# A decode step on one core: 256 rows of w4 as eight four-row loads ahead of w3

## The chip, the cores and the metric

One core of a Trainium2 chip runs the whole program. The metric is the device time of one execution in microseconds; the median of three runs of the kernel before is 193.53 us (193.38 to 193.78).

## The reference

A pre-norm block for one new token of eight sequences: attention over the last 2048 cached positions, and an MLP. Only these lines matter (`_B_ref` with S = 1 makes the shifted branch `hs` zero, so w1 and w2 are not read):

```python
# attention: q from x (8x512) by wq (512x4096); 32 heads, 8 kv heads, W = 2048 of 8192 positions
scores = einsum("bhqd,bhkd->bhqk", q, k) * Dh ** -0.5
o = einsum("bhqk,bhkd->bhqd", softmax(scores), v).reshape(B, Sq, Hq * Dh) @ wo
# MLP: w3 is 512x1792, w4 is 1792x512
h2 = gelu(layernorm(x1) @ w3) @ w4        # x1 = x + 0
# whole
h = x + attention(layernorm(x)); out = h + B_ref(layernorm(h))
```

All tensors are bf16. The key and value caches that are read make 67 MB of the 79 MB.

## The kernel before

Every engine has its own list of operations (`PE`, `AC`, `DV`, `PO`, `SP`), written out by hand in the order in which they are recorded; an operation waits on the counts of others or on a load's semaphore. All large loads go out on SyncE's queue in one order: wq, then 32 loads of keys and values of 2 MB (128 rows of 16 KB), four loads of wo of 1 MB, two of w3 (`sem_w3`), four of w4 (`sem_w4`), all through the helper at L199. Keys and values go through a ring of eight slots in SBUF (`ring`); a load into a slot waits until TensorE has taken what was there. w3 and w4 go into two slots of that ring.

Per slot of keys TensorE transposes (L325), ScalarE and VectorE evict (L334, L336), and TensorE makes the scores (L345). The softmax of one sequence is spread over following steps; GpSimd expands the probabilities (L384). The values are multiplied at L445, and after the last sequence at L454.

The tail is written in this order. `reorder` (L534 to L540) places the attention's output for the product with wo. `pe_wo` (L548) makes that product in four parts, one for each load of wo. Between them `stream(n)` (L596) has TensorE run n products that nobody reads, 512 columns wide. Sums for the layer norm follow (L685 to L700), then `uT`, the input of the MLP, whose tile GpSimd clears at L684. The product with w3 (L710) is made in two halves, one for each load of w3, over 14 chunks of 128 features; the results lie in two PSUM tiles, 8 chunks 64 columns wide and 6 chunks 32 wide. VectorE scales them (`g_x`, L738), ScalarE applies the GELU (`gT`, L741). TensorE adds the residual into the output's PSUM tile (`pe_fin`, L747), then the product with w4 (L755): two products for a chunk, side by side in two column groups of TensorE. Eviction (L775, L776) and the store (L779) end the program.

w4 is loaded in groups of 8, 3, 2 and 1 rows per partition, so that a group of r rows serves r chunks:

```python
w4_chunks += [slice(f0 + i, f0 + 128 * r, r) for i in range(r)]
dma(SP, w4_sb[:, lo:lo + r, :].rearrange("p r n -> p (r n)"),
    B_w4[f0:f0 + 128 * r, :].rearrange("(p r) n -> p (r n)", r=r), sem, w_free[1] if lo == 0 else None)
```

x_sb, the eight rows of the input, is loaded on ScalarE's queue by itself, the output is stored on SyncE's.

Of the kernel before, what the change touches and what calls it, by code (L numbers as in the profile page):

```python
# [11 lines left out]
B = 8  # L12
D = 512
# [9 lines left out]
FC = F // 128  # L23
KC = D // 128
EPS = 1e-5

NS = 8
NKT = 3
# [39 lines left out]
def bass_sequential_preLN__sliding_block_cached__mixer_s_mlp__decode_kernel(  # L68
# [23 lines left out]
    with es:  # L92
        sb = lambda shape, dtype, name: es.enter_context(nc.sbuf_tensor(name, shape, dtype))
        ps_t = lambda shape, dtype, name: es.enter_context(nc.psum_tensor(name, shape, dtype))
        S = lambda name: es.enter_context(nc.semaphore(name))
# [4 lines left out]
        ident_b = sb([128, 128], dt.bfloat16, "ident_b")  # L100
# [16 lines left out]
        QH, RW = H // 8, 8  # L117
# [12 lines left out]
        P4_sb = sb([128, 512, 4], dt.bfloat16, "P4_sb")  # L130
# [17 lines left out]
        half = sb([128, 2], dt.float32, "half")  # L148
# [38 lines left out]
        O_ps, O2_ps = (ps_t([128, 512], dt.float32, n) for n in ("O_ps", "O2_ps"))  # L187
# [3 lines left out]
        sem_wo = [S(f"sem_wo{i}") for i in range(NWO)]  # L191
        sem_x, sem_wq, sem_out = (S(n) for n in ("sem_x", "sem_wq", "sem_out"))
        sem_w3 = [S(f"sem_w3{i}") for i in range(2)]
        sem_w4 = [S(f"sem_w4{i}") for i in range(4)]
# [64 lines left out]
        e = PE.op(pe_xT, e_xln, e_idb)  # L259
# [22 lines left out]
        e = PE.op(pe_qT, *e_qr)  # L282
# [18 lines left out]
        place = {l: n for n, l in enumerate(quads)}  # L301
        taken = {}
# [123 lines left out]
        e_acc, e_oT = {}, {}  # L426
# [75 lines left out]
        v3 = lambda t: t.rearrange("p (n b) -> p n b", b=B)  # L502
        vr = lambda t: t.rearrange("p (n b) -> p b n", b=B)

        def bc(t):
            a = t[:, :]
            return bass.AP(tensor=a.tensor, offset=a.offset, ap=[a.ap[0], [0, KC], [1, B]])
# [82 lines left out]
            if p >= 7 + LQK + 7 and (p - 7 - LQK - 7) % 8 == 0:  # L590
                softmax_5((p - 7 - LQK - 7) // 8)

        def stream(n):
            def f(e):
                for _ in range(n):
                    ins = e.matmul(O2_ps[:, :], ident_b[:, :], kT_sb[:, (NG - 1) % NKT, 0:512], start=True, stop=True)  # L596
                return ins
            if n:
                PE.op(f, e_acc[NV - 4])
# [37 lines left out]
        pick_rest(14, 1)  # L637
        finish(13)
        pick_rest(14, 2, 3)
        stream(4)  # L640
        pv(60)
        finish(14)
        pv(61, 62, 63)

        e_oR = reorder()
        stream(3)
        for n in range(NWO):
            pe_wo(n, e_oR, e_oz)
            stream((0, 4, 4, 1)[n])


        dma(SP, wq_v, A_wq.rearrange("(p k) n -> p k n", k=KC), sem_wq)
        for l in loads:
            what, b, j = l
            if what == "wo":
                n, qh = b, QH // NWO
# [4 lines left out]
            n = place[l]  # L661
# [4 lines left out]


        w_free = [taken[quads[n - NS]] for n in (len(quads), len(quads) + 1)]
        for a, sem in enumerate(sem_w3):
            dma(SP, w3_sb[:, 2 * a:2 * (a + 1), :].rearrange("p r f -> p (r f)"),  # L670
                B_w3[256 * a:256 * (a + 1), :].rearrange("(p r) f -> p (r f)", r=2), sem, w_free[0])

        FH = 8
        w4_chunks, w4_ends, f0 = [], [], 0
        for r, sem in zip((8, 3, 2, 1), sem_w4):
            lo = len(w4_chunks)
            w4_chunks += [slice(f0 + i, f0 + 128 * r, r) for i in range(r)]
            dma(SP, w4_sb[:, lo:lo + r, :].rearrange("p r n -> p (r n)"),
                B_w4[f0:f0 + 128 * r, :].rearrange("(p r) n -> p (r n)", r=r), sem, w_free[1] if lo == 0 else None)
            w4_ends.append(lo + r)  # L680
            f0 += 128 * r
        assert len(w4_chunks) == FC

        e_uz = PO.op(lambda e: e.memset(uT, 0.0), e_PT[LAST, 3])  # L684
        e_d = DV.op(lambda e: e.tensor_tensor(v3(hd[:, :]), hT, v3(xc[:, :]), ALU.add), e_wo[-1], e_xc[0])  # L685
# [6 lines left out]
        e_u = DV.op(lambda e: e.scalar_tensor_tensor(uT[:, :, 0:B], bc(msum), -1.0 / D, v3(hd[:, :]),  # L692
                                                     ALU.mult, ALU.add), e_ms, e_uz)
# [9 lines left out]
        y_ps, NY = [kbank[0], kbank[2]], (64, 32)  # L703

        def pe_w3(half, lo, hi, *waits):
            def f(e):
                for fc in range(lo, hi):
                    n, f = divmod(fc, FH)
                    for kc in (2 * half, 2 * half + 1):
                        ins = e.matmul(y_ps[n][:, f * NY[n]:(f + 1) * NY[n]], w3_sb[:, kc, w4_chunks[fc]],  # L710
                                       uT[:, kc, 0:NY[n]], start=(kc == 0 and f == 0), stop=(kc == KC - 1),
                                       skip_group_check=True)
                return ins
            return PE.op(f, *waits)
        pe_w3(0, 0, FC, e_u, (sem_w3[0], 16), e_scale[LAST, 1], e_acc[NV - 2])
        stream(1)
        e_y = [pe_w3(1, 0, FH, (sem_w3[1], 16)), pe_w3(1, FH, FC)]

        e = AC.op(lambda e: e.activation(s2[:, :], vsum[:, :], ACT.Sqrt, bias=eps2[:, :], scale=(1.0 + EPS) / D), e_vs)  # L719
        e1 = AC.op(lambda e: e.activation(s1[:, :], vsum[:, :], ACT.Sqrt, bias=eps1[:, :], scale=1.0 / D))  # L720
# [14 lines left out]
        for n in range(2):  # L735
            fn = (FH, FC - FH)[n]
            cs = slice(n * FH * B, (n * FH + fn) * B)
            e = DV.op(lambda e, n=n, cs=cs, fn=fn: e.tensor_tensor(v3(g_x[:, cs]),   # L738
                y_ps[n][:, 0:fn * NY[n]].rearrange("p (f w) -> p f w", w=NY[n])[:, :, 0:B], bcf(r2, fn),
                                                                   ALU.mult), e_y[n], e_r2)  # L740
            e_gT.append(AC.op(lambda e, cs=cs: e.activation(gT[:, cs], g_x[:, cs], ACT.Gelu_apprx_tanh), e))  # L741
        z_ps = S_ps[1]

        def rows(e, w, rhs, start=False, stop=False):
# [6 lines left out]
        def pe_w4(lo, hi, *waits):  # L751
            def f(e):
                for fc in range(lo, hi):
                    for a in range(2):
                        ins = e.matmul(z_ps[64 * a:64 * a + B, 0:256], gT[:, fc * B:(fc + 1) * B],  # L755
                                       w4_sb[:, fc, 256 * a:256 * (a + 1)].rearrange("p (j r) -> p r j", r=2),
                                       start=False, stop=(fc == FC - 1), tile_position=(0, 64 * a), skip_group_check=True)
                return ins
            return PE.op(f, *waits)

# [4 lines left out]
            return ins  # L765

        PE.op(pe_fin, e_fin, e_exp[LAST], e_scale[LAST, 1])
        stream(2)
        for n, hi in enumerate(w4_ends):
            e_z = pe_w4(w4_ends[n - 1] if n else 0, hi, (sem_w4[n], 16), e_gT[0 if hi <= FH else 1])  # L770
        e_out = []
        for a in range(2):
            src = z_ps[64 * a:64 * a + B, 0:256].rearrange("p (r j) -> p r j", r=2)
            dst = out_sb[:, 256 * a:256 * (a + 1)].rearrange("p (j r) -> p r j", r=2)
# [38 lines left out]
```

## Time and profile before

| | |
|---|---|
| median of 3 runs | 193.53 us (193.38 to 193.78) |
| the profiled execution | 193.76 us, its span 192.3 us |
| TensorE busy, products / weight loads | 159.8 us (2108) / 101.8 us (2108) |
| VectorE, ScalarE, GpSimd busy | 103.8, 84.4, 35.8 us |
| HBM read | 79.18 MB, 412 GB/s over the span |
| granted TensorE clock | 1.0 throughout |

The span is the profiled part of the execution; the rest of its time lies around it. Times in the profile's rows are microseconds from the span's start. A row of instructions gives the line of the kernel, the engine, the operation, output and inputs, and in brackets the idle time ahead of it with what ended it.

### The profile page before, as it was taken

What the parts mean: (1) busy time and instruction counts of PE and PEld (TensorE: products, weight loads), DVE (VectorE), ACT (ScalarE), POOL (GpSimd) and SP (SyncE); (2) the same over time, 40 slices, a digit from 0 to 9 for tenths busy, and PEclk for the clock granted to TensorE, in tenths of its full rate; (3) what the DMA queues carried; (4) which work ended last, traced back from release to release, by engine and by line L of the source; (5) the groups of instructions that cost most, each with busy time, mean ns of one, the idle gap of its engine ahead of it and who ended that gap; (6) DMA issues with size and microseconds to landing.
All of it is one profiled execution on the core that took longest, in us unless ns stands there. A gap on an engine that the chain in (4) does not pass through costs nothing.

```text
span 192.3 us, 4741 instructions
## 1 busy us (share of the span) xinstructions
PE 159.8 (83%) x2108; PEld 101.8 (53%) x2108; DVE 103.8 (54%) x256; ACT 84.4 (44%) x102; POOL 35.8 (19%) x44
## 2 busy tenths in 40 slices
PE   0028999789998989998999797979998998898795
PEld 0015767567665555655656464646565653366472
DVE  7702656367457654665475546554765456552050
ACT  5002776946744544454444532454445423530040
POOL 8000000350520080008000800052004402400000
PEclk9999999999999999999999999999999999999999
DMA  6999999999999999999999999999999999999992
GB/s 220 436 423 436 433 416 433 426 428 423 436 429 433 429 433 423 426 429 431 433 423 433 429 433 429 429 433 426 424 426 429 429 433 433 423 416 430 418 381 77
DMA packets 6244, 79.47 MB, mean 413 GB/s; under 512 B 705, under 2 KB 849, under 8 KB 1361
## 3 DMA queue, kind: packets, MB, share of 16 engines
q1 hardware_dynamic: 6208, 79.18, 97.0%
q8 instruction: 16, 0.26, 0.5%
q10 hardware_dynamic: 16, 0.01, 0.0%
q14 instruction: 4, 0.02, 0.0%
HBM read 79.18 MB, written 0.01 MB: 412 GB/s over the span
## 4 chain that ended last, share of the span: by engine, by line
DMA 78%; PE 16%; DVE 2%; SPq 2%; issue 1%; ACT 0%
DMA ring<-in_A_k_cache_dram 63%; DMA ring<-in_B_w_dram 16%; PE kT_ps L325 8%; PE O_ps L445 3%; PE S_ps L345 3%; SPq L199 2%; DVE kT_sb L336 1%; PE sm L394 1%; PE sm L496 1%; DVE pT_sb L407 1%; PE S_ps L755 0%; DVE mcol L356 0%; ACT P_sb L775 0%; PE sm L360 0%; PE sm L370 0%
## 5 line engine op out<-in xcount | busy, mean ns | idle before, releaser
L334 ACT ACTIVATE kT_sb<-kT_ps 128x1024 bf16<-128x1024 bf16 x64 | 65.2, 1023 | 65.4 <-PE kT_ps L325 65.4
L325 PE MATMUL kT_ps<-ident_p,ring 128*128 128x128 bf16 x1024 | 68.3, 220 | 9.0 <-DMA ring<-in_A_k_cache_dram 7.6
L336 DVE COPY kT_sb<-kT_ps 128x1024 bf16<-128x1024 bf16 x64 | 44.3, 692 | 48.9 <-PE kT_ps L325 48.9
L325 PEld LDWEIGHTS kT_ps<-ident_p,ring 128*128 128x128 bf16 x1024 | 57.7, 98 | 22.5 <-DMA ring<-in_A_k_cache_dram 10.5
L384 POOL TENSOR_TENSOR P_sb<-P_sb,mask_b 128x512 bf16<-128x512 bf16 x30 | 31.2, 1070 | 129.2 <-ACT P_sb L374 120.1
L445 PE MATMUL O_ps<-ring,pT_sb 128*64 128x512 bf16 x208 | 31.6, 390 | 0.0
L345 PE MATMUL S_ps<-kT_sb,qwin 128*32 128x512 bf16 x256 | 26.0, 390 | 0.0
L345 PEld LDWEIGHTS S_ps<-kT_sb,qwin 128*32 128x32 bf16 x256 | 6.8, 93 | 16.3 <-issue 14.4
L394 PE MATMUL sm<-ident_s,P_sb 128*128 128x128 bf16 x120 | 11.6, 219 | 2.0 <-DVE pT_sb L407 0.7
L407 DVE COPY pT_sb<-sm 128x512 bf16<-128x512 bf16 x28 | 11.6, 415 | 1.1 <-PE sm L394 1.1
L445 PEld LDWEIGHTS O_ps<-ring,pT_sb 128*64 128x64 bf16 x208 | 7.7, 108 | 6.1 <-issue 1.6
L394 PEld LDWEIGHTS sm<-ident_s,P_sb 128*128 128x128 bf16 x120 | 7.7, 97 | 4.5 <-issue 3.6
L480 DVE SCALAR_TENSOR_TENSOR acc<-O_ps,own_f,acc 128x128 f32<-128x128 f32 x24 | 8.4, 350 | 0.8
L268 PE MATMUL S_ps<-wbig,xlnT 128*32 128x512 bf16 x32 | 3.4, 596 | 5.3 <-DMA wbig<-in_A_wq_dram 5.3
L374 ACT ACTIVATE P_sb<-S_ps,negcol 128x512 bf16<-128x512 f32 x8 | 5.5, 687 | 3.0 <-DVE negcol L373 3.0
L254 PE MATMUL sm<-ident_b,xln_b 8*128 8x8 bf16 x4 | 0.3, 174 | 7.6 <-DVE xln_b L223 7.6
L496 PEld LDWEIGHTS sm<-sum_f,acc 128*128 128x128 f32 x20 | 3.0, 188 | 6.3 <-DVE pT_sb L407 3.3
L356 DVE TENSOR_REDUCE mcol<-S_ps 128x1 f32<-128x512 f32 x8 | 5.5, 689 | 1.5 <-PE S_ps L345 1.5
L480 DVE SCALAR_TENSOR_TENSOR iota_f<-O_ps,own_f,iota_f 128x128 f32<-128x128 f32 x15 | 5.2, 348 | 1.5 <-ACT iota_f L483 1.2
L596 PE MATMUL O_ps<-kT_sb,ident_b 128*128 128x512 bf16 x21 | 5.8, 379 | 0.0
L435 DVE TENSOR_TENSOR oT_all<-sm,rL 128x16 bf16<-128x16 f32 x15 | 3.4, 229 | 4.4 <-PE sm L496 4.3
L719 ACT ACTIVATE s<-vsum,eps 128x8 f32<-128x8 f32 x1 | 0.3, 301 | 11.8 <-DVE vsum L699 11.8
(123 smaller groups left out, 109.8 us busy)
## 6 DMA issues: line engine op xcount, KB each, us to landing
ring<-in_A_k_cache_dram SPq DMA_DIRECT2D x16, 2048.0 KB, 30.7
ring<-in_A_v_cache_dram SPq DMA_DIRECT2D x16, 2048.0 KB, 26.8
wbig<-in_A_wq_dram SPq DMA_DIRECT2D x1, 4096.0 KB, 12.3
wbig<-in_A_wo_dram SPq DMA_DIRECT2D x4, 1024.0 KB, 29.9
ring<-in_B_w_dram SPq DMA_DIRECT2D x2, 896.0 KB, 34.9
ring<-in_B_w_dram SPq DMA_DIRECT2D x1, 1024.0 KB, 32.1
ring<-in_B_w_dram SPq DMA_DIRECT2D x1, 384.0 KB, 30.3
ring<-in_B_w_dram SPq DMA_DIRECT2D x1, 256.0 KB, 30.5
```

The costliest lines, as they stand in the source:

```text
L325: ins = e.matmul(kT_ps[m % 3][:, c * 128:(c + 1) * 128], ring[:, s, n * DH:(n + 1) * DH], ident_p[:, :], is_transpose=True)
L334: e_lo[i] = AC.op(lambda e: e.activation(kT_sb[:, i % NKT, 0:1024], kT_ps[2 * i % 3][:, :], ACT.Copy), e_Tlo[i], e_QK.get(i - NKT))
L336: e_hi[i] = DV.op(lambda e: e.tensor_copy(kT_sb[:, i % NKT, 1024:2048], kT_ps[(2 * i + 1) % 3][:, :]), e_Thi[i], e_QK.get(i - NKT))
L345: ins = e.matmul(S_ps[b % 2][32 * h:32 * (h + 1), :], qwin[:, b, 4 * j + h, w0:w0 + 32], kT_sb[:, i % NKT, :].rearrange("p (c h k) -> p h ...
L356: e_max[b] = DV.op(lambda e: e.tensor_reduce(mcol[:, :], S_ps[b % 2][:, :], AX.X, ALU.max), e_QK[8 * b + 7], e_mT.get(b - 1))
L374: e_exp[b] = AC.op(lambda e: e.activation(P_sb[:, :], S_ps[j][:, :], ACT.Exp, bias=negcol[:, j:j + 1], scale=1.0, accum_out=lcol[:, j:j + 1]),
L384: e_sp[b, r] = eng.op(lambda e, r=r, pb=pb, mb=mb: e.tensor_tensor(P4_sb[:, 128 * r:128 * (r + 1), :], pb, mb, ALU.mult), e_exp[b], e_PT.g ...
L394: ins = e.matmul(buf[:, x * 128:(x + 1) * 128], P4_sb[:, 32 * c:32 * (c + 1), :].rearrange("p k h -> p (k h)"), ident_s[:, :], is_transpos ...
L407: e_pT[b, r] = DV.op(lambda e: e.tensor_copy(dst, pT_ps[:, :]), e_PT[b, r], free)
L445: ins = e.matmul(bank(w)[64 * t:64 * (t + 1), :], pT_sb[:, b % NB3, c, 64 * j:64 * (j + 1)], ring[:, s, :].rearrange("p (a c d) -> p c a d ...
L480: e_part[w] = eng.op(lambda e: e.scalar_tensor_tensor(dst, src, own, dst, ALU.mult, ALU.add), e_part[w], e_PV[4 * w + 3])
L596: ins = e.matmul(O2_ps[:, :], ident_b[:, :], kT_sb[:, (NG - 1) % NKT, 0:512], start=True, stop=True)
```

## The change

A free ring slot (that of the last load of keys) takes 256 of w4's 1792 rows, the first ones, laid out over 64 partitions with eight rows each. GpSimd first clears that area and makes a small selection matrix `near` from the identity. Eight loads of four partitions (8 KB each) then fill the rows, on SyncE's queue between wo and w3: load n writes partitions p, p+4, p+8, p+12 with p = 32(n // 4) + n mod 4. 32 of the 64 partitions are filled so; the others stay zero. The remaining 1536 rows of w4 come in groups of 5, 4, 2 and 1 rows per partition.

The product with w3 now has three PSUM parts: the two chunks for the first 256 features, the five of w4's first group, the other seven. Of the first part, g is put into the layout of the new rows by 16 small products (`pe_near`) and a copy (`gn`), and the product with these rows is eight pairs of TensorE products, placed behind those of w4's first group. The filler products become 128 columns wide, in other numbers; the one between the halves of w3 goes from one to three of 512, and the two ahead of w4 go.

```diff
-        def stream(n):
+        def stream(n, w=512):
...
-        stream(4)
+        stream(12, 128)
         pv(60)
...
         e_oR = reorder()
-        stream(3)
+        stream(12, 128)
         for n in range(NWO):
             pe_wo(n, e_oR, e_oz)
-            stream((0, 4, 4, 1)[n])
+            stream((0, 14, 16, 4)[n], 128)
...
+        side = ring[:, place["k", LAST, 1] % NS, :]
+        near_sb = side[0:64, 0:RW * D].rearrange("p (r n) -> p r n", r=RW)
+        near = side[:, RW * D:RW * (D + 32)].rearrange("p (r n) -> p r n", r=RW)
+        e_nz = PO.op(lambda e: e.memset(near_sb, 0.0), taken["k", LAST, 1])
+        e = PO.op(lambda e: e.memset(near, 0.0))
+        e_near = PO.op(lambda e: e.tensor_copy(near[:, :, 0:16], ident_b[:, :].rearrange("p (n r) -> p r n", r=RW)), e)
+        for n in range(RW):
+            p, f = 32 * (n // 4) + n % 4, 128 * (n // 4) + RW * (n % 4)
+            dst = near_sb[p:p + 13:4].rearrange("p r n -> p (r n)")
+            a = B_w4[f:f + RW, :]
+            dma(SP, dst, bass.AP(tensor=a.tensor, offset=a.offset, ap=[[4 * RW * D, 4], [1, RW * D]]), sem_near, e_nz)
         for a, sem in enumerate(sem_w3):
             dma(SP, w3_sb[:, 2 * a:2 * (a + 1), :].rearrange("p r f -> p (r f)"),
...
-        for r, sem in zip((8, 3, 2, 1), sem_w4):
+        for r, sem in zip((5, 4, 2, 1), sem_w4):
...
+        w3_parts = ((0, NN, 64), (NN, w4_ends[0], 64), (w4_ends[0], FC, 32))
...
-        pe_w3(0, 0, FC, e_u, (sem_w3[0], 16), e_scale[LAST, 1], e_acc[NV - 2])
-        stream(1)
-        e_y = [pe_w3(1, 0, FH, (sem_w3[1], 16)), pe_w3(1, FH, FC)]
+        for n in range(3):
+            pe_w3(0, n, e_u, (sem_w3[0], 16), e_scale[LAST, 1], e_acc[NV - 2])
+        stream(3)
+        e_y = [pe_w3(1, n, (sem_w3[1], 16)) for n in range(3)]
...
+        gn_ps = kbank[1][0:64, 0:RW * B]
+        gn = P4_sb[0:64, 64:80, :].rearrange("p k h -> p (k h)")
+
+        def pe_near(e):
+            for r in range(RW):
+                for t in range(NN):
+                    ins = e.matmul(gn_ps[32 * t:32 * (t + 1), r * B:(r + 1) * B], near[:, r, :], gT[:, t * B:(t + 1) * B],
+                                   start=True, stop=True, tile_position=(0, 32 * t), skip_group_check=True)
+            return ins
...
         PE.op(pe_fin, e_fin, e_exp[LAST], e_scale[LAST, 1])
-        stream(2)
+        e = PE.op(pe_near, e_gT[0], e_near)
+        e_gn = DV.op(lambda e: e.tensor_copy(gn, gn_ps), e, e_PT[LAST, 3])
         for n, hi in enumerate(w4_ends):
-            e_z = pe_w4(w4_ends[n - 1] if n else 0, hi, (sem_w4[n], 16), e_gT[0 if hi <= FH else 1])
+            e_z = pe_w4(gT, w4_sb, w4_ends[n - 1] if n else NN, hi, (sem_w4[n], 16), e_gT[1 if n == 0 else 2])
+            if n == 0:
+                pe_w4(gn, near_sb, 0, RW, e_gn, (sem_near, 16 * RW))
```

More of the change, by code (lines that the diff above doesn't have):

```diff
@@ L193, in bass_sequential_preLN__sliding_block_cached__mixer_s_mlp__decode_kernel @@
         sem_w3 = [S(f"sem_w3{i}") for i in range(2)]
+        sem_near = S("sem_near")
         sem_w4 = [S(f"sem_w4{i}") for i in range(4)]
@@ L591, in bass_sequential_preLN__sliding_block_cached__mixer_s_mlp__decode_kernel @@
                 softmax_5((p - 7 - LQK - 7) // 8)
-        def stream(n):
+        def stream(n, w=512):
             def f(e):
                 for _ in range(n):
-                    ins = e.matmul(O2_ps[:, :], ident_b[:, :], kT_sb[:, (NG - 1) % NKT, 0:512], start=True, stop=True)
+                    ins = e.matmul(O2_ps[:, 0:w], ident_b[:, :], kT_sb[:, (NG - 1) % NKT, 0:w], start=True, stop=True)
                 return ins
@@ L671, in bass_sequential_preLN__sliding_block_cached__mixer_s_mlp__decode_kernel @@
                 B_w3[256 * a:256 * (a + 1), :].rearrange("(p r) f -> p (r f)", r=2), sem, w_free[0])
-        FH = 8
-        w4_chunks, w4_ends, f0 = [], [], 0
-        for r, sem in zip((8, 3, 2, 1), sem_w4):
+        NN = 2
+        w4_chunks, w4_ends, f0 = [slice(128 * i, 128 * (i + 1)) for i in range(NN)], [], 128 * NN
+        for r, sem in zip((5, 4, 2, 1), sem_w4):
             lo = len(w4_chunks)
@@ L678, in bass_sequential_preLN__sliding_block_cached__mixer_s_mlp__decode_kernel @@
             dma(SP, w4_sb[:, lo:lo + r, :].rearrange("p r n -> p (r n)"),
-                B_w4[f0:f0 + 128 * r, :].rearrange("(p r) n -> p (r n)", r=r), sem, w_free[1] if lo == 0 else None)
+                B_w4[f0:f0 + 128 * r, :].rearrange("(p r) n -> p (r n)", r=r), sem, w_free[1] if lo == NN else None)
             w4_ends.append(lo + r)
@@ L701, in bass_sequential_preLN__sliding_block_cached__mixer_s_mlp__decode_kernel, with pe_w3 @@
                                                       ALU.mult, ALU.add))
-        y_ps, NY = [kbank[0], kbank[2]], (64, 32)
-        def pe_w3(half, lo, hi, *waits):
+        y_ps = [sm[:, 128:128 + 64 * NN], kbank[0], kbank[2]]
+        def pe_w3(half, n, *waits):
+            lo, hi, w = w3_parts[n]
             def f(e):
                 for fc in range(lo, hi):
-                    n, f = divmod(fc, FH)
                     for kc in (2 * half, 2 * half + 1):
-                        ins = e.matmul(y_ps[n][:, f * NY[n]:(f + 1) * NY[n]], w3_sb[:, kc, w4_chunks[fc]],
-                                       uT[:, kc, 0:NY[n]], start=(kc == 0 and f == 0), stop=(kc == KC - 1),
+                        ins = e.matmul(y_ps[n][:, (fc - lo) * w:(fc - lo + 1) * w], w3_sb[:, kc, w4_chunks[fc]],
+                                       uT[:, kc, 0:w], start=(kc == 0 and fc == lo), stop=(kc == KC - 1),
                                        skip_group_check=True)
@@ L734, in bass_sequential_preLN__sliding_block_cached__mixer_s_mlp__decode_kernel @@
         e_gT = []
[L735 to L739, printed above, removed]
+        for n, (lo, hi, w) in enumerate(w3_parts):
+            cs = slice(lo * B, hi * B)
+            e = DV.op(lambda e, n=n, cs=cs, fn=hi - lo, w=w: e.tensor_tensor(v3(g_x[:, cs]),
+                y_ps[n][:, 0:fn * w].rearrange("p (f w) -> p f w", w=w)[:, :, 0:B], bcf(r2, fn),
                                                                    ALU.mult), e_y[n], e_r2)
             e_gT.append(AC.op(lambda e, cs=cs: e.activation(gT[:, cs], g_x[:, cs], ACT.Gelu_apprx_tanh), e))
+        gn_ps = kbank[1][0:64, 0:RW * B]
[6 more added lines that the diff above has]
+            return ins
         z_ps = S_ps[1]
@@ L749, in rows, with pe_w4 @@
             return ins
-        def pe_w4(lo, hi, *waits):
+        def pe_w4(g, w, lo, hi, *waits):
             def f(e):
@@ L754, in f @@
                     for a in range(2):
-                        ins = e.matmul(z_ps[64 * a:64 * a + B, 0:256], gT[:, fc * B:(fc + 1) * B],
-                                       w4_sb[:, fc, 256 * a:256 * (a + 1)].rearrange("p (j r) -> p r j", r=2),
-                                       start=False, stop=(fc == FC - 1), tile_position=(0, 64 * a), skip_group_check=True)
+                        ins = e.matmul(z_ps[64 * a:64 * a + B, 0:256], g[:, fc * B:(fc + 1) * B],
+                                       w[:, fc, 256 * a:256 * (a + 1)].rearrange("p (j r) -> p r j", r=2),
+                                       start=False, stop=(w is w4_sb and fc == FC - 1), tile_position=(0, 64 * a), skip_group_check=True)
                 return ins
```

## The prediction

> **What bounds the kernel now.** First the page: its transfers by slice and the chain that ended last.
>
> ```profile
> span 192.3 us, 4741 instructions
> DMA  6999999999999999999999999999999999999992
> GB/s 220 436 423 436 433 416 433 426 428 423 436 429 433 429 433 423 426 429 431 433 423 433 429 433 429 429 433 426 424 426 429 429 433 433 423 416 430 418 381 77
> DMA 78%; PE 16%; DVE 2%; SPq 2%; issue 1%; ACT 0%
> ```
>
> The kernel is a stream of 79 MB at about 430 GB/s, and the chain is 78% transfers. A change pays only if the last bytes land earlier and TensorE is then ready for them. The last two slices, 381 and 77 GB/s, are not full. The table of busy time by windows shows why (last columns: granted clock, DMA share of 16 engines, GB/s):
>
> ```profile
> 186.00:186.50 0.50, 0.50 (x12) 0.50 (x11) 0.00 (x0) 0.00 (x0) 0.00 (x0) 1.00 1.02 404
> 186.50:187.00 0.50, 0.50 (x18) 0.47 (x18) 0.23 (x1) 0.00 (x0) 0.00 (x0) 1.00 0.60 242
> 187.00:188.00 1.00, 0.90 (x13) 0.29 (x14) 0.21 (x1) 0.50 (x2) 0.00 (x0) 1.00 0.59 227
> 188.00:189.00 1.00, 1.00 (x16) 0.61 (x16) 0.00 (x0) 0.00 (x0) 0.00 (x0) 1.00 0.50 185
> 189.00:189.50 0.50, 0.36 (x8) 0.18 (x6) 0.00 (x0) 0.00 (x0) 0.00 (x0) 1.00 0.40 143
> ```
>
> From 186.5 us half of the DMA engines have nothing left, while the other half work on until about 190. Every load gives each engine the same bytes, so something else holds that half back. The table of queues names it:
>
> ```profile
> q1 hardware_dynamic: 6208, 79.18, 97.0%
> q8 instruction: 16, 0.26, 0.5%
> q10 hardware_dynamic: 16, 0.01, 0.0%
> q14 instruction: 4, 0.02, 0.0%
> ```
>
> q8 has 16 packets of 16 KB of instructions. The trace's single packets show that one takes 0.88 to 0.97 us of its engine and slows the packet behind it. On one engine a packet begins some 4 ns before the last one ends, so I could follow each engine: the fetches go round eight engines, two each, and make those some 2.9 us late; a ninth, with two 8 KB packets of q14, is about 1.7 us late; seven are free or nearly. The sixteen landings of the last load, w4's last 128 KB, agree: seven at 186.7 to 187.5 us, one at 188.36, eight at 189.6 to 190.12.
>
> The TensorE timeline (weight loads: start, length) shows what the late eight hold up:
>
> ```profile
> 185.57 1.35 PEld L710 LDWEIGHTS kT_ps<-P_sb,ring 128*128 128x128 bf16 x28 [0.66 <-DMA ring<-in_B_w_dram]
> 187.99 0.77 PEld L755 LDWEIGHTS S_ps<-ring,gT 128*8 128x8 bf16 x16 [0.59 <-DMA ring<-in_B_w_dram]
> 189.20 0.21 PEld L755 LDWEIGHTS S_ps<-ring,gT 128*8 128x8 bf16 x6 [0.44 <-DMA ring<-in_B_w_dram]
> 189.82 0.09 PEld L755 LDWEIGHTS S_ps<-ring,gT 128*8 128x8 bf16 x4 [0.41 <-DMA ring<-in_B_w_dram]
> 190.13 0.09 PEld L755 LDWEIGHTS S_ps<-ring,gT 128*8 128x8 bf16 x2 [0.22 <-DMA ring<-in_B_w_dram]
> ```
>
> Each group of w4 products waits for its load; the last pair starts at 190.13, 0.01 us after the last landing. All behind it (eviction, store) is unchanged.
>
> **The change: where the bytes go.** x_sb is a load of eight rows; its queue q10 has 16 packets: eight of data, eight that count the semaphore. So a load of eight rows uses eight engines, and one of four rows should use four. Then the eight new loads put 64 KB on each of four engines: 8 packets of 8 KB at 0.305 us (0.309 each, 4 ns of overlap) and 8 semaphore packets at 5 ns, 2.48 us. The other loads of w4 shrink from 14 to 12 KB per partition, 8 partitions an engine: 16 KB less on every engine, 0.61 us by the spacing of 16 KB packets (0.611 less 0.004). So twelve engines end 0.61 us earlier, the four 2.48 - 0.61 = 1.87 us later. If the four are free ones, they end at 187.46 + 1.87 = 189.33 at most, the late ones at 190.12 - 0.61 = 189.51, which is the new last landing.
>
> [...]
>
> **Issue.** The new loads wait on POOL: its last product of L384 ends at 165.3, then a memset of 64x4096 (3.29 us for 128x3840 at L213, so 3.5), end 168.8. uT's memset, queued behind it and two short ones, moves from 167.4 to about 169.5; it is needed at 183.3. On SP the w3 and w4 issues queue behind the wait: eight at 0.48 us (spacing of the wo issues) to 172.7, the six others to about 176, if the queue takes them (it held one back 11 us before, with ten loads outstanding). The free engines finish wo at 178.0. Cost nothing; cover 2 us for the last issue, 9 us for the first; without it each us late is a us lost.
>
> **TensorE.** On late engines w3's second half still lands at 185.56, the new loads not being theirs. stream(3) before it takes 3 x 0.213 = 0.64 from 184.84, so 185.48: hidden, by 0.08. The other fillers become 128 wide: 12 to 16 at 0.05 to 0.06 us against 3 or 4 at 0.213, no longer than before and each in front of a load it waits for anyway; nothing. Then, by starts in the rows of before: y, 14 products of 64 columns at 0.060 and 14 of 32 at 0.0255, to 186.80 (186.87 before); pe_fin's eight to 187.1. The 16 products that place g aren't in the trace: lower bound L534 (same 32-column weights, 0.35 us for 32, so 0.18 for 16), upper bound 0.96 (0.060 each, as y's). I take 0.2, L534 having the same form. Their copy starts 0.26 later (as L738 behind y) and takes 0.21 and 0.05 to be seen: 187.8. Meanwhile five pairs of w4's first group (landed at 187.98 before, with 24 KB or 0.9 us more per engine, so 187.1 now), at 0.113 a pair (spacing at L755): 187.3 to 187.9. Then 8 + 4 + 2 + 1 = 15 pairs, the new eight included; the last starts 14 x 0.113 = 1.58 later, at 189.5. That is level with the landing at 189.51, and all the removed waits of L755 are filled. At the upper bound it is 190.2 and nothing is gained; with 0.1 to 0.2 us of unseen semaphore time, 189.7.
>
> **Sum.** The last pair moves from 190.13 to 189.53 (transfers) or 189.7 (TensorE): 0.43 to 0.60 us, I take 0.5. The profiled execution took 193.76 us (span 192.3 and 1.4 around it), 0.23 over the median of 193.53; on it 193.26, on the median 193.0.
>
> **Rivals.**
> *One of the four carries fetches (slower).* Of the eight engines that took x_sb's rows, my tracking gives five free or nearly, one with q14's two packets, two with q8's two. Which four a four-row load takes, the trace doesn't say. For: by blind choice it would be likely. Against: the two with q8 come next to each other in the round of eight and may as well be at the far end of the order. It decides as soon as one of the four is late by over 0.2 us. With a q8 engine w3's second half lands at 185.56 + 2.48 = 188.04; the whole TensorE tail moves by as much, last pair 192.05: +1.9, 195.4 us. With the q14 engine it lands at 183.98 (its landing before) + 2.48 = 186.46, 0.9 later; last pair 190.4 to 190.6: 193.9.
> *The tail stays where it is.* TensorE has 70 products more (42 fillers, 16 to place g, 12 for the new rows), each with a weight load: 4216 + 140 = 4356 instructions. The 16 fetches came about every 256, so a 17th falls due at 4352, in the last products. Lag from that count to the packet was 2.7 us in the last two, which puts it past the end; where it comes sooner it holds a late engine by up to 1 us. With that, or placing g nearer its upper bound, 0 to 0.35 us is left: 193.2 to 193.5.
> [...]
> *Small loads cost one by one (slower).* If each new load paid a round trip (the store's 0.9 us from issue to landing), eight would take 7.2 us on the four engines: 186.7 + 7.2 - 0.61 = 193.3 for their end, +3.2, 196.7. Against: the semaphore packets of queued loads take 9 ns, and the next data follows with no gap.
> [...]
> *The loads spread over all sixteen.* Then no engine gains, w3 lands 0.6 later, TensorE's last pair is at 190.1 to 190.3: 193.6. x_sb's packets speak against it.
>
> **How the numbers follow.** Forecast 0.52; q8 engine 0.14; q14 engine 0.11; tail 0.15; cost one by one 0.03; spread 0.05. The forecast's own range is 192.9 to 193.15. 192.8 (lowest run 193.38 less 0.6) to 194.2 takes in all but the q8 engine and the cost one by one. About 0.2%, 0.39 us, is what a measurement of this kernel can tell from no change: faster by more 0.52 (the forecast), within 0.20 (tail, spread), slower 0.28.
>
> **What would show it.** Right: the share of DMA engines stays at about 1.0 to past 188.5 and drops steeply; w3's second half is taken up at 185.6 and no w4 group waits long; the last pair starts near 189.5. Wrong: L710's second half starting at 186.5 or 188 (a loaded engine was late already), a DMA share of a quarter or less trailing past 190, a 17th q8 packet before 189.5, or the copy of g starting after 188.2. Gaps between packets before 186 us would mean that the issues came too late.

## The result and the profile after: slower by about a microsecond

The changed kernel takes 194.59 us (median of 6 runs, 194.30 to 195.12) against 193.59 for the kernel before in the same runs (6, 193.38 to 193.78). The ratio is 1.0057 [1.0039, 1.0075]: slower, where 193.0 was forecast, and above the range given. The profiled execution took 194.56 us. Two kernels further down (e13, e14) had executions 3 to 4 us longer at a lower granted clock, and their ratios leave these out.

The page of the changed kernel, its transfers by slice, its chain and its queues:

```profile
span 192.9 us, 4897 instructions
DMA  6999999999999999999999999999999999999981
GB/s 219 435 431 435 428 425 431 425 426 428 428 431 428 431 428 428 435 418 430 431 428 428 428 431 435 425 435 426 425 421 435 435 428 431 425 415 426 423 362 48
q1 hardware_dynamic: 6272, 79.18, 96.7%
q8 instruction: 17, 0.28, 0.5%
q14 instruction: 3, 0.02, 0.0%
DMA 44%; PE 40%; DVE 5%; POOL 4%; ACT 3%; SPq 3%; issue 1%
```

The last two slices have become emptier (362 and 48 GB/s, from 381 and 77): the end did not fill up. The chain now goes 40% through TensorE, but it is one path among several of nearly equal length, and most of the difference lies far ahead of the change. Queue q8 has its 17th packet; by the single packets it begins at 188.90 us.

The table of busy time by windows (last columns: granted clock, DMA share, GB/s):

```profile
186.00:186.50 0.50, 0.49 (x3) 0.00 (x0) 0.00 (x0) 0.00 (x0) 0.00 (x0) 1.00 0.77 315
187.00:187.50 0.50, 0.50 (x20) 0.50 (x17) 0.17 (x1) 0.16 (x1) 0.00 (x0) 1.00 0.75 309
188.50:189.00 0.50, 0.50 (x10) 0.23 (x6) 0.16 (x1) 0.00 (x0) 0.00 (x0) 1.00 0.50 170
189.00:189.50 0.50, 0.50 (x12) 0.38 (x12) 0.00 (x0) 0.00 (x0) 0.00 (x0) 1.00 0.06 25
190.00:190.50 0.50, 0.50 (x12) 0.39 (x12) 0.00 (x0) 0.00 (x0) 0.00 (x0) 1.00 0.03 10
```

This has two signatures at once. From 186 to 188 us the share is 0.73 to 0.78, about twelve engines, where before it was 0.60 from 186.5 on, nine or ten: four engines got new rows, but only about three of them had been idle. And a share of 0.06 is one engine of sixteen, and it goes on alone from 189 to past 190. The sixteen landings of w4's last load show the same: four at 186.2 to 186.5 us, eleven at 188.48 to 189.40, one at 190.58. Before there were seven early ones, a single one at about 188.3 and eight late ones. Less the 0.61 us by which w4's loads shrank, the single one would stand at 187.7; none does. So three of the four loaded engines were early ones, and the fourth is the one that stood alone.

The timeline of the changed kernel (a row of products, then weight loads: start, length) shows what that one engine held up on its way:

```profile
184.75 0.28 PE L724 MATMUL sm<-P_sb,ring 128*128 128x64 bf16 x4 [1.11 <-DMA ring<-in_B_w_dram]
186.80 0.17 PEld L724 LDWEIGHTS sm<-P_sb,ring 128*128 128x128 bf16 x4 [0.81 <-DMA ring<-in_B_w_dram]
188.35 0.43 PEld L778 LDWEIGHTS S_ps<-ring,gT 128*8 128x8 bf16 x10
189.01 0.77 PEld L778 LDWEIGHTS S_ps<-ring,P_sb 64*8 64x8 bf16 x16 [0.23 <-issue]
190.01 0.69 PEld L778 LDWEIGHTS S_ps<-ring,gT 128*8 128x8 bf16 x14 [0.23 <-issue]
```

L724 is the product with w3 (L710 before). Its second half is taken up at 186.80 us, 1.23 later than before, and waits for a transfer: fifteen of its sixteen landings are there by 185.54 and the last at 186.76. Its first half, too, waits until 184.75, for a last landing at 184.61. w4's first group starts at 188.35, its last landing being at 188.30. From there TensorE has no wait left. The last seven pairs start at 190.01, so the last of them, six spacings of 0.113 us on, at 190.69 (190.13 before).

So the last pair is 0.56 us later in the profiled executions. The kernel before has a span of 192.1 or 192.2 us in most later runs, where its profiled execution had 192.3; the changed one has 192.7 to 193.6 us. That makes about 0.8 us inside the span. The rest lies around it: time less span is 1.60 us on the mean over the changed kernel's runs and 1.33 over those of the kernel before.

### The profile page after: what moved, and what is told of

The parts are those of the page before. It is cut to its first block, busy times and chain, and to the rows that moved or that the text cites. A ratio compares the mean times of both kernels' runs of the same rounds, so it can differ in the third digit from the quotient of the medians.

```text
span 192.9 us, 4897 instructions
## 1 busy us (share of the span) xinstructions
PE 162.8 (84%) x2178; PEld 107.0 (55%) x2178; DVE 103.8 (54%) x258; ACT 84.7 (44%) x103; POOL 39.9 (21%) x47
## 3 DMA queue, kind: packets, MB, share of 16 engines
q1 hardware_dynamic: 6272, 79.18, 96.7%
## 4 chain that ended last, share of the span: by engine, by line
DMA 44%; PE 40%; DVE 5%; POOL 4%; ACT 3%; SPq 3%; issue 1%
DMA ring<-in_A_k_cache_dram 31%; PE kT_ps L326 20%; DMA ring<-in_B_w_dram 6%; DMA wbig<-in_A_wq_dram 6%; PE S_ps L346 6%; PE O_ps L446 6%; SPq L200 3%; DVE kT_sb L337 3%; PE S_ps L269 2%; PE sm L395 2%; POOL ring L673 2%; POOL P_sb L385 2%; PE S_ps L778 1%; ACT kT_sb L335 1%; PE sm L497 1%
## 5 line engine op out<-in xcount | busy, mean ns | idle before, releaser
L326 PE MATMUL kT_ps<-ident_p,ring 128*128 128x128 bf16 x1024 | 70.8, 224 | 5.7 <-DMA ring<-in_A_k_cache_dram 4.4
L326 PEld LDWEIGHTS kT_ps<-ident_p,ring 128*128 128x128 bf16 x1024 | 60.5, 101 | 18.6 <-issue 8.8
L597 PE MATMUL O_ps<-kT_sb,ident_b 128*128 128x128 bf16 (+1 forms) x63 | 5.5, 232 | 0.2 <-issue 0.2
```

What stands on the lines that cost most here:

```text
L326: ins = e.matmul(kT_ps[m % 3][:, c * 128:(c + 1) * 128], ring[:, s, n * DH:(n + 1) * DH], ident_p[:, :], is_transpose=True)
```

## The experiments

Three questions: which of the loaded engines is the late one, what a transfer ahead of w3 costs where no engine is late, and where the 0.27 us around the span come from. The theory at the start: one of the four engines that a four-row load uses is the one that q14's packets had made late. Rivals: any extra load ahead of w3 costs, or the added TensorE work does. "The change" in a diff is the changed kernel; e5, e6, e9 and e12 edit the kernel before, which ran at 193.44 to 193.57 us beside all of these.

**e1_sixteen.** The same rows by two loads of sixteen adjacent partitions, so that each engine gets two packets:

```
-        for n in range(RW):            # eight loads, partitions p, p+4, p+8, p+12
...
+        for t in range(NN):            # two loads
+            dma(SP, near_sb[32 * t:32 * t + 16]..., B_w4[128 * t:128 * (t + 1), :]..., sem_near, e_nz)
```

> The same 256 rows by two loads of sixteen rows, so that all sixteen engines share them; all else as changed. Theory (one of the four engines of the four-row loads is the one with q14's two packets, and w3's second half waits for it): no engine gets more than before, the second half of w3 is taken up near 186.2 in place of 186.8, the last pair of w4 products starts at 190.1, time 193.6. Rival A (the added products, the copy and the fillers cost the time): 194.5, as changed. Rival B (each small load costs by itself): two loads in place of eight, 193.8.

Measured: 197.56 us (196.69 to 198.62), ratio 1.0206 [1.0180, 1.0233]. A miss by 4 us. The table by windows:

```profile
178.00:180.00 2.00, 1.13 (x39) 0.96 (x37) 0.00 (x0) 0.00 (x0) 0.00 (x0) 1.00 1.05 311
182.00:184.00 2.00, 1.19 (x36) 1.03 (x36) 0.18 (x1) 0.00 (x0) 0.00 (x0) 1.00 0.94 170
186.00:188.00 2.00, 1.29 (x29) 1.29 (x30) 1.22 (x7) 1.31 (x2) 0.00 (x0) 0.50 0.99 403
```

The engines are all busy, yet they move 311 and then 170 GB/s instead of 430. Packets of 8 KB, 309 ns in the kernel before, take up to 908 in this stretch, those of 7 KB (272) up to 876. From 185.0 to 191.8 us the granted clock is 0.50, and three filler products of 512 columns take 1.44 us, where the changed kernel takes 0.81. That where the engines write decided here, and not their number, is a reading that e7, e8, e11 and e13 test.

**e4_six_rows.** Five loads of six adjacent partitions and one of two, 32 partitions in all, no memset ahead of them:

```
+        for lo, n in ((0, 6), (6, 6), (12, 6), (18, 6), (24, 6), (30, 2)):
+            dma(SP, near_sb[lo:lo + n]..., B_w4[RW * lo:RW * (lo + n), :]..., sem_near, taken["k", LAST, 1])
```

> All 256 rows laid out over 32 adjacent partitions and loaded by five loads of six rows and one of two, so that six engines share them (five or six rows each in place of eight); the clearing of the rows falls away, the selection of g has the same 16 products. Theory: w3's second half lands on the q14 engine at 183.98 + 1.5 to 1.8 = 185.5 to 185.8, the last landing is at 189.5, last pair 189.5 to 189.7, time 193.0 to 193.2. Rival A: 194.5, the same products being there. Rival B: six loads for eight, 194.3.

Measured: 197.41 us (196.46 to 197.70), ratio 1.0192 [1.0173, 1.0212]. The same miss: 8 KB packets take up to 700 ns near 179.3 us, and the granted clock is 0.50 from 185.0 to 191.9.

**e2_behind_w3.** The eight loads of the change, behind w3's two instead of ahead.

```
+        for a, sem in enumerate(sem_w3): ...   # w3 first
         for n in range(RW): ...
-        for a, sem in enumerate(sem_w3): ...
```

> The eight four-row loads issued behind w3 in place of ahead of it. Theory: w3's second half is taken up at 185.6 again, and the last pair follows the last landing on the loaded q14 engine, 190.45: last pair 190.46, time 194.2 to 194.4. Rival A: 194.5, with w4's pairs back to back behind the copy of g and no wait for a load. Rival B: the last landing past 190.45, time 194.5 or more.

Measured: 194.38 us (194.17 to 196.31), ratio 1.0068 [1.0042, 1.0095]. The time is as expected. The timeline:

```profile
185.81 0.17 PEld L724 LDWEIGHTS sm<-P_sb,ring 128*128 128x128 bf16 x4 [0.82 <-DMA ring<-in_B_w_dram]
188.37 0.43 PEld L778 LDWEIGHTS S_ps<-ring,gT 128*8 128x8 bf16 x10 [1.06 <-DMA ring<-in_B_w_dram]
190.03 0.66 PEld L778 LDWEIGHTS S_ps<-ring,gT 128*8 128x8 bf16 x14 [0.23 <-issue]
```

w3 is in time again (taken up at 185.81 us, 186.80 in the change), and now w4's first group waits 1.06 us: its landings are all there by 187.27 us but one, at 188.32. The wait has moved to the load that is now behind the new rows. The end came by another path than was said: the last landing is at 190.56 (190.45 expected), but the last pair does not wait for it. From 188.37 us on TensorE works through its w4 products without a wait, as in the change, and starts the last pair at 190.03 + 6 x 0.113 = 190.71.

**e3_half.** Half of the rows: four loads instead of eight, w4's groups 6, 4, 2, 1.

```
-        for n in range(RW):
+        for n in range(4):
...
-        NN = 2
+        NN = 1
-        for r, sem in zip((5, 4, 2, 1), sem_w4):
+        for r, sem in zip((6, 4, 2, 1), sem_w4):
```

> Half of the rows: 128 by four four-row loads, w4's others in groups of 6, 4, 2 and 1. Theory: the q14 engine has w3's second half by 183.98 + 1.24 = 185.2, so it is taken up at 185.6; the late engines have 8 KB less and end at 189.8; last pair 189.85, time 193.3. Rival A: half of the added products, half of the loss: 194.0. Rival B: half of the loads, 194.0.

Measured: 193.74 us (193.63 to 195.16), ratio 1.0019 [1.0006, 1.0032]. The timeline:

```profile
185.78 0.11 PEld L724 LDWEIGHTS sm<-P_sb,ring 128*128 128x128 bf16 x2 [0.97 <-DMA ring<-in_B_w_dram]
187.61 0.55 PEld L778 LDWEIGHTS S_ps<-ring,gT 128*8 128x8 bf16 x12 [0.23 <-DMA ring<-in_B_w_dram]
189.39 0.66 PEld L778 LDWEIGHTS S_ps<-ring,gT 128*8 128x8 bf16 x14 [0.23 <-issue]
```

Of the 0.27 us over the kernel before, 0.24 lie around the span (time less span 1.57). Four packets fewer on the late engine, and w3's second half is taken up 1.02 us earlier than in the change. What was missed is the end: from 187.61 on TensorE works without a break, to the last pair at 189.39 + 6 x 0.113 = 190.07. The eight pairs of 32 rows replace one chunk of w4: seven pairs more, 0.8 us at 0.113 each, against a last landing that comes 0.4 us earlier than in the profile of the kernel before (189.72, about 190.1).

**e5_fillers and e6_semaphore.** The kernel before with the change's fillers of 128 columns alone (those around w3 and w4 stay as they were), and with an unused semaphore alone.

```
-            stream((0, 4, 4, 1)[n])               # e5, with its two neighbours
+            stream((0, 14, 16, 4)[n], 128)
```

```
+        sem_near = S("sem_near")                  # e6
```

> The kernel before with the changed fillers alone (12, 12, 0, 14, 16 and 4 products of 128 columns). Theory (the loss is the loaded engine's): 193.5, no change. Rival A (fillers and added instructions cost): a part of the 1.0 us, with the time outside of the span grown from 1.3 to 1.6 us if the instructions make that.

> The kernel before with one semaphore more that nothing uses, for the 0.3 us by which the changed kernel's time outside of its span exceeds that of before. Theory: 193.5 to 193.8 with the span unchanged; the upper end if the semaphore makes the 0.3 us, the lower if it doesn't. Rival A: 193.5.

Measured: 193.54 us, ratio 1.0002 [0.9994, 1.0011], and 193.47 us, 1.0000 [0.9992, 1.0009]. Neither costs anything, and time less span stays at 1.32 to 1.33 us. The 17th q8 packet came in e5 as well (189.21 us), without harm.

**e7_six_ports.** Loads of six rows, as in e4, but four partitions apart.

```
+        for l in range(6):
+            p, cnt = 32 * (l // 4) + l % 4, 6 if l < 5 else 2
+            dma(SP, near_sb[p:p + 4 * cnt - 3:4]..., B_w4[RW * 6 * l:RW * (6 * l + cnt), :]..., sem_near, taken["k", LAST, 1])
...
```

> The 256 rows by five loads of six rows and one of two, as in e4_six_rows, but into partitions four apart as in the changed kernel (24 products place g, with no clearing of the rows). Theory: adjacent partitions made e4's transfers slow; with partitions four apart packets of 8 KB take 0.31 us again; w3's second half lands on the q14 engine at 185.5 to 185.8, w4's first group by 187.5, the late engines end at 189.5, last pair 189.6 to 189.8; time 193.1, or 193.4 with 0.3 us more outside of the span. Rival (loads of six rows are slow whatever the partitions): 197. Rival A (the added products cost it): 194.5.

Measured: 194.73 us (194.20 to 195.09), ratio 1.0065 [1.0051, 1.0078]. The packets are back at 309 and 272 ns, so the places of the rows were the cause in e4. The time was missed: w3's second half is taken up at 186.68 us, after a single landing at 186.64, where the others are there by 185.69.

```profile
186.68 0.17 PEld L729 LDWEIGHTS sm<-P_sb,ring 128*128 128x128 bf16 x4 [0.81 <-DMA ring<-in_B_w_dram]
```

By the single packets this is not the engine that was late in the change. That one begins its five new packets at 179.48 us and has the last landed at 181.36; in the change 4.29 us passed from there to its landing of w3's second half (182.47 to 186.76), which gives 185.65 here, within the 185.5 to 185.8 expected. Another engine ends wo only at 180.43, as the eight late ones do, then takes five new packets of its own, the last landed at 182.33; 4.29 us on, that is 186.62. So six engines take in one of those that q8's fetches made late, and four do not. That the time came out near that of the change is chance.

**e8_sixteen_ports.** One load of 32 rows, four partitions apart over all 128, two packets on each of sixteen engines.

```
+        dma(SP, near_sb[0:125:4]..., B_w4[0:32 * RW, :]..., sem_near, taken["k", LAST, 1])
```

> The 256 rows by one load of 32 rows into partitions four apart over all 128, so that sixteen engines share them, two rows each (32 products place g, the eight new pairs span 128 partitions). Theory: no engine has more bytes than before; w3 lands 0.6 later everywhere, its second half is taken up at 186.2, the last pair is at 190.2 to 190.4: 193.7 to 194.0, no gain and no loss but the 0.3 us outside. Rival A: 194.5. [...]

Measured: 193.86 us (193.59 to 194.66), ratio 1.0025 [1.0014, 1.0035]. The time is as expected; the last pair comes 0.2 us earlier than was said. The timeline:

```profile
186.25 0.17 PEld L722 LDWEIGHTS sm<-P_sb,ring 128*128 128x128 bf16 x4 [0.88 <-DMA ring<-in_B_w_dram]
189.97 0.09 PEld L777 LDWEIGHTS S_ps<-ring,gT 128*8 128x8 bf16 x2 [0.15 <-DMA ring<-in_B_w_dram]
```

With twice as many products to place g and all the new pairs, the last pair comes at 189.97 and the span is 192.2 us, the value before. So neither the bytes ahead of w3 nor the added products make the loss inside the span; that of the change needs one engine that gets more than it can take. What is left here, 0.26 us, lies around the span.

**e9_three_memsets.** In the runs so far time less span had the mean 1.33 us in kernels with 58 instructions on GpSimd (before, e5, e6) and with 66 (e7), and 1.57 to 1.69 with 60 (e4) and 61 (the others, the change among them). So the kernel before, with three memsets that nothing reads:

```
+        for i in range(3):
+            PO.op(lambda e, i=i: e.memset(side[:, 8 * i:8 * i + 8], 0.0), taken["k", LAST, 1])
```

> The kernel before, with three small memsets more on GpSimd (nothing reads them). Theory A: the 0.27 us more outside the span (mean 1.33 us in the kernel before and in the runs with 58 and 66 GpSimd instructions, 1.57 to 1.69 us in those with 60 and 61) hangs on how many instructions GpSimd's program has: with 61 the time outside becomes 1.60, the span stays 192.1 to 192.3, the time is 193.75 (ratio 1.0014). Rival: it comes from the new loads or products; then nothing moves: 1.33 outside, 193.48.

Measured: 193.74 us (193.64 to 193.90), ratio 1.0015 [1.0006, 1.0023]; time less span 1.59 us, spans 192.1 to 192.3. This settles that part: three idle instructions on GpSimd cost the 0.27 us. In the kernels with 66 the single packets show one more 8 KB fetch of q14 in the record, at 192.0 to 192.7 us (196.2 in e13's longer execution); in the others none after 135 us. That a fetch at the end of the program falls differently is a reading of it that no run tests.

**e10_split_group.** e3 with w4's first group of six rows as 3 + 3, the new pairs behind the second of them, and five more memsets (66 instructions).

```
-        for r, sem in zip((6, 4, 2, 1), sem_w4):
+        for r, sem in zip((3, 3, 4, 2, 1), sem_w4):
...
-            if n == 0:
+            if n == 1:
                 pe_w4(gn, near_sb, 0, RW, e_gn, (sem_near, 16 * 4))
```

> The version of e3_half (128 rows by four loads of four partitions), its first w4 group of six rows split into two of three, g's eight copied products behind the second of them, and five small memsets more on GpSimd (66 instructions as in e7_six_ports). Theory: in e3_half TensorE worked without a break from 187.61 us, when the landing of six rows let it go, to the last pair at 190.07, while the last load landed at 189.7; a group of three lands about 0.5 us sooner and TensorE starts when its g is ready, about 187.15; last pair at 189.7 to 189.8, span 192.0, time outside 1.33 instead of 1.57: 193.2 to 193.3 (ratio 0.9985 to 0.999). Rival: one more load on the queue, or the copied g, which is ready at 187.75, holds TensorE up: last pair still at 190.0, 193.5. Rival: the time outside doesn't follow the memsets: 0.25 us more on either.

Measured: 193.31 us (193.05 to 193.62), ratio 0.9989 [0.9980, 0.9998]; time less span 1.37 us. Faster than both kernels, by 0.1%, which is less than the 0.39 us that the prediction names, with an interval that ends just short of 1. The timeline of its profiled execution, the slowest of its runs:

```profile
186.00 0.11 PEld L727 LDWEIGHTS sm<-P_sb,ring 128*128 128x128 bf16 x2 [1.10 <-DMA ring<-in_B_w_dram]
187.85 0.21 PEld L781 LDWEIGHTS S_ps<-ring,gT 128*8 128x8 bf16 x6 [0.32 <-DMA ring<-in_B_w_dram]
190.00 0.09 PEld L781 LDWEIGHTS S_ps<-ring,gT 128*8 128x8 bf16 x2 [0.17 <-DMA ring<-in_B_w_dram]
```

TensorE's w4 products start at 187.26, 0.35 us sooner than in e3, and the last pair waits for its load again, as in the kernel before.

**e12_split_only.** The kernel before with its first group of eight as 4 + 4.

```
-        for r, sem in zip((8, 3, 2, 1), sem_w4):
+        for r, sem in zip((4, 4, 3, 2, 1), sem_w4):
```

> The kernel before with nothing changed but its first w4 group of eight rows, split into two loads of four; no rows ahead of w3. Theory: the gain of e10_split_group (193.31 against 193.48) needs both the rows moved ahead of w3 and the smaller first group; in the kernel before the last pair waits for the last load (190.13), which the split doesn't bring forward, so TensorE starts at 187.9 or sooner and waits longer behind: last pair at 190.1, time 193.4 to 193.55 (ratio 1.000). Rival: the split alone earns it: last pair at 189.9 or sooner, 193.3, and the moved rows are worth nothing.

Measured: 193.53 us (193.47 to 193.63), ratio 1.0004 [0.9995, 1.0013]. The time is as expected: the split alone does nothing. In the timeline the time that it wins is lost in the next wait, 0.68 us where the kernel before had 0.44; the wait behind it is as it was (0.43, 0.41 before):

```profile
188.93 0.21 PEld L755 LDWEIGHTS S_ps<-ring,gT 128*8 128x8 bf16 x6 [0.68 <-DMA ring<-in_B_w_dram]
189.57 0.09 PEld L755 LDWEIGHTS S_ps<-ring,gT 128*8 128x8 bf16 x4 [0.43 <-DMA ring<-in_B_w_dram]
```

Its last pair starts at 189.87, where the rival had 189.9 or sooner. But e5, e6 and e9, whose loads are those of the kernel before, have theirs at 190.00, 190.10 and 189.87, so that a tenth or two in one profiled execution says nothing by itself, here or in e3, e8 and e10.

**e11_two_rows.** e3's rows by eight loads of two partitions, p and p + 4: eight packets on each of two engines.

```
-        for n in range(4): ...
+        for n in range(8):
+            p = n % 4 + 8 * (n // 4)
+            dst = near_sb[p:p + 5:4].rearrange("p r n -> p (r n)")
```

> As e3_half (128 rows of w4 ahead of w3; groups of 6, 4, 2 and 1), but by eight loads of two partitions: eight packets of 8 KB on each of two engines, as many on an engine as the change under study has on each of four. Theory: the loss of the change is one engine among its four that instruction packets make late; if it is not among the first two, the two loaded engines have time to spare, w3's second half is taken up by 185.6 us and the last pair comes at 190.0 as in e3_half: 193.6 to 193.75. If it is among the first two, it is as late as in the changed kernel: w3's second half at 186.7 to 186.8, last pair at 190.6, 194.2 to 194.4. Rival: eight such packets ahead of w3 make any engine too late, free or not: two landings of w3's second half at 186.3 or later.

Measured: 194.71 us (194.58 to 194.96), ratio 1.0065 [1.0051, 1.0079]. It told nothing of the engines, since something else came in. The table by windows:

```profile
180.50:181.00 0.50, 0.37 (x7) 0.20 (x4) 0.00 (x0) 0.00 (x0) 0.00 (x0) 1.00 0.89 184
181.00:181.50 0.50, 0.00 (x0) 0.00 (x0) 0.00 (x0) 0.00 (x0) 0.00 (x0) 1.00 1.04 217
```

All engines are busy at half the rate: 8 KB packets take 628 ns at the median from 180 to 182 us, 7 KB ones 513. The first four new packets of each engine (to partitions 0 to 3 and 4 to 7) came at 0.31 us, the last four (8 to 11 and 12 to 15) at 0.62. The rows of e1 (twice 16) and e4 (32) also went to adjacent partitions. Why rows in these places slowed all transfers is not shown by any view here; e13 changes the places alone.

**e13_own_partitions and e14_own_split.** e11 with the rows in partitions 0 to 7 and 32 to 39 in place of 0 to 15 (16 products place g in place of eight, and four idle memsets bring GpSimd to 66 instructions), and that with e10's split.

```
-            p = n % 4 + 8 * (n // 4)
+            p, f = n % 4 + 32 * (n // 4), RW * (n % 4 + 8 * (n // 4))
```

> [...] The late engine is the third or fourth, so w3's second half is taken up by 185.7 us, the last pair comes at 189.9 to 190.1, time outside 1.33: 193.3 to 193.5. Rival: the late engine is the first or second: w3's second half at 186.5 to 186.8, 194.2 to 194.4. Rival: something other than the partitions slowed the packets in e11_two_rows: 633 ns again, 194.4.

> e13_own_partitions with the first w4 group split into two of three rows, as in e10_split_group. In e10_split_group w3's second half was taken up at 186.00 us, the landing on the late engine with four more packets; here by 185.7, so that g is ready 0.3 us sooner and TensorE has its w4 products done as the loads land. Last pair at 189.7 to 189.9, 193.15 to 193.3 (ratio 0.9985 to 0.999). Rival: the last landing sets the end in both, 189.9 to 190.0: 193.3 as in e10_split_group.

Measured: e13 193.48 us, against 193.57 for the kernel before beside it, ratio 0.9994 [0.9985, 1.0003]; e14 193.47 us, 0.9995 [0.9982, 1.0009]. e13's executions lie at 193.27 to 193.71 and one at 197.69, which is the profiled one: its granted clock was 0.50 from 167.5 to 174.3 us and TensorE ran late from there on, so only its transfers are used. e14's lie at 193.13 to 193.50, with one at 194.45 and two at 196.72 and 197.40. Packets are at 309 and 272 ns in both, the new rows are in by 180.95 (e13), and w3's second half lands by 185.62 (e13) and 185.80 (e14). So the places were what slowed e11, and eight packets on each of two engines leave w3 almost where it was (185.53 before), where four loaded engines leave it at 186.76: the late engine is one of the other two, if a two-row load uses two of the four, which no view here shows. e14's gain was expected at 0.2 to 0.3 us and isn't shown, though four of its executions lie at 193.13 to 193.19; in its profile the end is set by the landings, as its rival had it:

```profile
189.96 0.09 PEld L783 LDWEIGHTS S_ps<-ring,gT 128*8 128x8 bf16 x2 [0.23 <-DMA ring<-in_B_w_dram]
```

## Why the prediction was wrong, step by step

**Where it held.** Half of the engines idle at the end, four-row loads on four engines, no round trip per load: the window shares and the packets bear this out: q1 has 64 more (6272 against 6208), which is four of data and four for the semaphore in each of eight loads, and on one engine they follow each other by 0.31 us. The late eight finished earlier: eleven landings, theirs among them, of the last load are there by 189.40, where 189.51 was worked out. GpSimd's memset ended at 168.65 (168.8 said), the fourteen issues at 176.66 (176). The tail was sized well: from w3's second half to the last pair 3.96 us were worked out (185.57 to 189.53), and 3.89 are measured (186.80 to 190.69). The 0.1 to 0.2 us of semaphore time in TensorE's sum is the author's margin, taken from no run; in the change the pairs of w4 products start 0.113 us apart but for two places, at the first new pair and behind the last, where it is 0.21. e5 and e8 bear out that the fillers and the products that place g cost nothing inside the span.

**The step that failed** is "if the four are free ones". One was not: the rival with the q14 engine came true, which had 0.11. It put w3's second half at 183.98 + 2.48 = 186.46; the landing was at 186.76, because that engine was some 0.3 us later in this execution. It put the last pair at 190.4 to 190.6; it was at 190.69. What it did not have is w3's first half, late by 1.2 us without consequence, and w4's first group, whose landing at 188.30 came as TensorE had just placed g. That q14's packets are what made this engine late is read from the packets alone, and no run varies them: in the kernel before, the engine is 0.8 us behind the first at the end of a load near 130 us and 1.5 us behind at the end of the next but one, and q14's packet of 134.64 us lies between.

**The chance was the larger error.** The tracking in the prediction had five engines free or nearly, one with q14's packets and two with q8's, among the eight that x_sb uses. If a four-row load takes four of these eight, which no view here shows, then four picked blindly are all free in 5 of 70 ways, hold the q14 engine but no q8 engine in 10, and hold a q8 engine in 55. The text granted "by blind choice it would be likely", and gave 0.52 to the case that its own count puts at 0.07. e13 beside the change shows how to learn it without a view of engine numbers, load two engines, then four, and e7 adds that with six there is one of q8's.

**The size was short by 0.7 us** even for the rival (193.9 against 194.59). The 1.4 us around the span were carried over unchanged, a term that no step priced: with three GpSimd instructions more they are 0.27 us longer (e9), with eight more they are not. Most of the rest is the late engine, with the last pair at 190.69 where the rival had 190.4 to 190.6, and a profiled execution of before, from which the moves were counted, that was 0.1 to 0.2 us over its usual span.

**Where the expected gain went.** Where the late engine holds up little or nothing (e3, e8, e13) it is not 0.5 us either. But e3 and e13 move half of the rows and e8 loads all sixteen engines: 256 rows on four engines that are all free were not run, so what the forecast promised for that case stays open. e8 and e3 end at 189.97 and 190.07: with even loads the late eight still land last (189.92 in e8), and with half of the rows TensorE becomes the bound. e10's smaller first group takes that bound off TensorE, and 0.17 us (193.48 to 193.31) is the most that any of these kernels gained; e14, with the same split, does not show it again.

## What to carry to other kernels

Before moving bytes to "free" DMA engines, find out which engines the new load will use and count the ways: here one of the four loaded engines was late already, w3's second half was taken up 1.23 us later for it, and with the new loads behind w3 (e2) w4's first group waited 1.06 us instead. Probes with two and with four loaded engines told more than a packet trace without engine numbers. Price what a change adds on engines off the path as well: a few instructions on GpSimd moved the end by 0.27 us.

## What the runs showed of the hardware that was not expected

- Where a small load put its rows slowed all transfers in two kinds of runs: 170 to 311 GB/s instead of 430 with adjacent partitions (e1), 184 to 217 with the last four rows of each of two engines in partitions 8 to 15 (e11). With the rows of e11 in partitions 0 to 7 and 32 to 39 (e13), or four partitions apart (the change, e7, e8), nothing of it is left. Why the places matter is not shown by any view here.
- In e1 and e4, behind such a stretch, the granted clock stood at 0.50 from about 185.0 to 191.8 us, and from w3's last landing to the last pair passed 5.0 us in e1 (188.70 to 193.72), against 3.9 in the change. What lowers the clock stays open: in the profile of the change it stood at 0.50 from 118.1 to 121.5 us too, with no slow transfers there.
- Time less span is 1.33 to 1.37 us with 58 or 66 GpSimd instructions and 1.57 to 1.69 with 60 or 61, so it does not simply grow with their number; e9 shows the step from 58 to 61 with nothing else changed.
